# Moving operands of the two feed-forward products kept as even and odd columns 4 KB apart and read alternately

## The chip, the cores and the metric

The kernel runs on one core of a Trainium2 chip. The metric is the device time of one execution in microseconds (us), as the median of several runs; a profile is one more execution, with the hardware profiler on.

## The reference, cut to what matters

A batch of 8 sequences of 576 tokens, with 8 heads of 64 numbers, goes through an attention of two parts: one over means of 4 tokens (144 x 144 scores a head), and a local one over the 7 nearest tokens. Their sum, as a matrix x of 4608 tokens by 512, goes through two dense layers:

```python
h = x @ w_in                                        # 4608 x 512 by 512 x 2048
g = np.maximum(h, 0.0) + alpha * np.minimum(h, 0.0)
return (g @ w_out).astype(np.float32)               # 4608 x 2048 by 2048 x 512
```

The inputs are 64-bit floats in memory; the kernel reads them as pairs of 32-bit words and builds 32-bit floats of the weights itself.

## The kernel before, in words

**The two products.** Every factor is held as a high part of type float32r (a rounded 32-bit type of TensorE) and a low part, the rest; a product is high*high + high*low + low*high. The tokens are cut in 18 chunks of T = 256, the 2048 columns of h in 16 blocks of 128, two to a step, so there are NS = 144 steps, 8 (NP) to a chunk. A step issues two groups on TensorE:

- `hidden` (L751) computes h for 2 blocks: 24 matmuls, in which a 128 x 128 piece of the first weights (`wi`, high or low) is the stationary operand and 256 tokens of x (`xT[c]`, tiles xh and xl) the moving one (L760).
- `product` (L805) adds two blocks of g times the second weights to the output: 12 matmuls, in which 128 tokens of g (gh or gl) are stationary and 512 columns of a row block of the second weights (`wo`, tiles woh and wol) move (L817).

The stationary operand is loaded ahead (rows PEld in the profile); the moving operand streams through the array, one column after another. In memory the 256 tokens of x for one of four row blocks, and the 512 columns of a `wo` block, lie next to each other, in 1 KB and 2 KB of a partition.

**Between the two groups** of a step lie ScalarE's `slopes` (L771, L775), VectorE's `larger` (L783), and `split`: ScalarE casts g to gh (L788), GpSimd subtracts it to gl (`sub`, L70).

**Who makes the operands.** `make` (L164) builds the weights from the raw words in five operations: ScalarE reads every second word (L187), VectorE assembles the bits in `temp` (L191 to L197), ScalarE writes the high part (L206 for `wo`), VectorE the low part (L214). For the later batches x is made in units of 192 tokens, on VectorE for the most part (L597 to L677). `place` (L682) then lets ScalarE write the high part (L691) and GpSimd the low part (L70). The first batch has its own code (L523 to L525), its last 64 tokens another (`place_rest`, L840).

**The order.** First comes the first batch's attention with most of the weights, about 100 us. After it every operation has a due time in units of steps (`at`), and the sorted list is issued as it stands, so each engine runs its instructions in that order. Transfers are issued by SyncE (SP) in the same order. The last raw blocks of weights (`load_raw`, L133, with fp = 6 and 7) have tiles in the pool `late`: for fp = 7 those that later hold the x tiles of every third chunk (xh and xl).

Of the kernel before, what the change touches and what calls it, by code (L numbers as in the profile page):

```python
# [51 lines left out]
def tile_attention_moe(ctx: ExitStack, tc: tile.TileContext, q, k, v, w_in, w_out, alpha, out):  # L52
# [13 lines left out]
    def f32(ap):  # L66
        return ap.bitcast(F32)
# [50 lines left out]


    wi, wo = ([[None] * 4, [None] * 4] for _ in range(2))  # L120
    for name, w in (("wi", wi), ("wo", wo)):
        for i, x in enumerate("hl"):
            w[i][0] = const.tile([128, 4, 512], F32R, name=f"{name}{x}0")

# [6 lines left out]
    def load_raw(which, fp, blocks=(0, 1)):  # L133
        raw = raws.setdefault((which, fp), {})
        if fp < NP - 2:
            raw[None] = one.tile([128, 1024, 2], I32, tag=f"slot{turns[0] % 3}", name=f"raw{which}_{fp}")
            raw[0], raw[1] = raw[None][:, 0:512], raw[None][:, 512:1024]
            turns[0] += 1
        src = (w_in, w_out)[which].bitcast(I32)
        for c in blocks:  # L140
            if fp < NP - 2:
                dst = raw[None][:, 512 * c:512 * c + 512]
            elif fp == NP - 2:
                dst = raw[c] = late.tile([128, 512, 2], I32, tag="prod", name=f"raw{which}_{fp}{c}", bufs=PB)
            else:
                dst = raw[c] = late.tile([128, 512, 2], I32, tag=f"x{'hl'[c]}", name=f"raw{which}_{fp}{c}")
            if which == 0:
                nc.sync.dma_start(dst.rearrange("p (k a) b -> p k (a b)", k=2),
                                  bass.AP(src.tensor, 256 * c * 2 * DF + 512 * fp, [[2 * DF, 128], [256 * DF, 2], [1, 512]]))
            else:  # L150
                row = 256 * fp + 128 * c
                nc.sync.dma_start(dst.rearrange("p a b -> p (a b)"), src[row:row + 128, :])

    def weight_tiles(which, n):
        if n == 0 or (wi, wo)[which][0][n] is not None:
            return
        w = (wi, wo)[which]
        for i, x in enumerate("hl"):
            tag = f"slot{2 * which + i}" if n == 3 else f"spare{8 - 4 * n + 2 * which + i}"
            w[i][n] = one.tile([128, 4, 512], F32R, tag=tag, name=f"w{'io'[which]}{x}{n}")  # L160

    def make(which, fp, c=None):  # L164
        n, half = divmod(fp, 2)
        cs = (0, 1) if c is None else (c,)
        k = len(cs) * (2 - which)
        w = (wi, wo)[which]
        st = {}

        def part(i, c):
            if which == 0:
                return w[i][n][:, 2 * cs[0]:2 * cs[-1] + 2, 256 * half:256 * half + 256]
            f = (2 * fp + c) % 4
            return w[i][n][:, f:f + 1]

        def magnitude():
            if not weights_temp:
                weights_temp.append(one.tile([128, 2, 1024], I32, tag="slot3", name="temp"))
            if c is None:  # L180
                t = weights_temp[0][:, turns[1] % 2]
            else:
                t = bank("ql"[turns[1] % 2], f"temp{which}{fp}{c}").bitcast(I32)
            turns[1] += 1
            st["raw"] = raws[which, fp].pop(c).rearrange("p (k a) b -> p k a b", k=k)
            st["t"] = t.rearrange("p (k a) -> p k a", k=k)
            nc.scalar.activation(f32(st["t"]), f32(st["raw"][:, :, :, 1]), AF.Abs)  # L187

        def reach():
            t = st["t"]  # L190
            nc.vector.tensor_scalar(f32(t), f32(t), W_MIN, W_MAX, op0=ALU.max, op1=ALU.min)  # L191
            nc.vector.tensor_scalar(t, t, 3, 0x3FFFFFF8, op0=ALU.logical_shift_left, op1=ALU.bitwise_and)

        def bits():
            t, hi, lo = st["t"], st["raw"][:, :, :, 1], st["raw"][:, :, :, 0]
            nc.vector.scalar_tensor_tensor(t, hi, -0x40000000, t, op0=ALU.bitwise_and, op1=ALU.bitwise_or)  # L196
            nc.vector.scalar_tensor_tensor(t, lo, 29, t, op0=ALU.logical_shift_right, op1=ALU.bitwise_or)  # L197

        def upper():
            weight_tiles(which, n)  # L200
            if which == 0:
                nc.scalar.copy(part(0, 0), f32(st["t"]))
            else:
                for i, c in enumerate(cs):
                    sg = sign[:, 2 * fp + c:2 * fp + c + 1]
                    nc.scalar.activation(part(0, c), f32(st["t"][:, i:i + 1]), AF.Copy, scale=sg)  # L206

        def lower():
            if which == 0:
                nc.vector.tensor_tensor(part(1, 0), f32(st["t"]), f32(part(0, 0)), op=ALU.subtract)  # L210
            else:
                for i, c in enumerate(cs):
                    sg = sign[:, 2 * fp + c:2 * fp + c + 1]
                    nc.vector.scalar_tensor_tensor(part(1, c), f32(st["t"][:, i:i + 1]), sg, f32(part(0, c)),  # L214
                                                   op0=ALU.mult, op1=ALU.subtract)

        return magnitude, reach, bits, upper, lower
# [136 lines left out]
    def operand(c):  # L354
        if c not in xT:
            pool = late if c % 3 == 2 else two
            xT[c] = [pool.tile([128, 4, T], F32R, tag=f"x{x}", name=f"x{x}{c}") for x in "hl"]
        return xT[c]


    def spans(pos, n):
# [7 lines left out]
    def first_batch(st):  # L369
# [55 lines left out]
        def pair(hp):  # L425
# [85 lines left out]
            for w0, nw in ((0, 4), (4, 4), (8, 1)):  # L511
                ps = pair_bank(FPV[hp][w0 // 4], f"fpv{hp}{w0}")
                for i in range(nw):
                    for e, r in enumerate(halves):
                        nc.tensor.matmul(ps[r, WIN * i:WIN * i + WIN], vw[hp][:, w0 + i, e, :],
                                         pT[:, w0 + i, 64 * e:64 * e + 64], start=True, stop=True)
                xs = rest[:, hp, :] if w0 == 8 else st.tile([128, 256], F32, tag="xs", name=f"fxs{hp}{w0}")
                nc.vector.tensor_tensor(
                    xs.rearrange("p (a r) -> p a r", r=4),
                    ps[:, 0:WIN * nw].rearrange("p (a r) -> p a r", r=4),  # L520
                    odf[:, 16 * w0:16 * (w0 + nw)].unsqueeze(2).to_broadcast([128, 16 * nw, 4]), op=ALU.add)
                if w0 < 8:
                    hi, lo = (t[:, hp, :] for t in operand(w0 // 4))  # L523
                    nc.scalar.copy(hi, xs)  # L524
                    nc.vector.tensor_tensor(lo, xs, f32(hi), op=ALU.subtract)  # L525
            yield

        return load_pair, load_windows, pair
# [43 lines left out]
    def local(u, t0, t1):  # L572
# [109 lines left out]
        def place(i, low):  # L682
            j0, nt = groups[i]
            xv = st["xf", i].rearrange("p a t s -> p a (t s)")
            at_ = 0
            for c, o, n in spans(192 * u + 32 * j0, 32 * nt):
                hi, lo = (t[:, :, o:o + n] for t in operand(c))
                if low:
                    sub(lo, xv[:, :, at_:at_ + n], f32(hi))
                else:  # L690
                    nc.scalar.copy(hi, xv[:, :, at_:at_ + n])  # L691
                at_ += n

        def put(i, t):
# [55 lines left out]

    def hidden(st):  # L751
        c, fp = divmod(st, NP)
        xh, xl = xT[c]
        ph = hs[st] = ps_h.tile([128, 2, T], F32, tag="ph", name=f"h{st}")
        for j in range(2):
            n, o = divmod(2 * fp + j, 4)
            i = 0
            for w, x in ((wi[0][n], xh), (wi[1][n], xh), (wi[0][n], xl)):
                for m in range(4):
                    nc.tensor.matmul(ph[:, j], w[:, m, 128 * o:128 * o + 128], x[:, m, :],  # L760
                                     start=(i == 0), stop=(i == 11))
                    i += 1

# [41 lines left out]
    def product(st):  # L805
# [7 lines left out]
        for j, i, m in order:  # L813
            f = 2 * fp + j
            n, o = divmod(f, 4)
            g, w = ((gh, 0), (gh, 1), (gl, 0))[i]
            nc.tensor.matmul(outs[c][m], g[:, j, 128 * m:128 * m + 128], wo[w][n][:, o, :],  # L817
                             start=(f == 0 and i == 0), stop=(f == NF - 1 and i == 2))

    def finish(c):  # L820
# [17 lines left out]
                (nc.sync if i % 2 == 0 else nc.scalar).dma_start(ap, sg[32 * i:32 * i + 32, :])  # L838

    def place_rest():  # L840
        hi, lo = (t[:, :, 0:S - 2 * T] for t in operand(2))
        nc.scalar.copy(hi, rest)
        sub(lo, rest, f32(hi))

# [47 lines left out]
    for w, fp, c in blocks:  # L894
        for lag, f in zip((-0.3, 0.0, 0.4, 0.95, 1.2), make(w, fp, c)):
            at(t + lag * D_DEC, f)
        t += D_DEC
        if w == 0 and fp >= NP - 2:
            at(t, load_raw, 1, fp, (c,))
    decoded = t  # L900
    for p in range(4 * (B - 1)):
        b, hp = 1 + p // 4, p % 4
# [87 lines left out]
```

## Time and profile before

| | |
|---|---|
| median of 3 runs | 999.41 us (998.8 to 1003.49) |
| span of the profiled execution | 995.7 us |
| median over that span | 3.7 us |
| busy TensorE / VectorE / ScalarE / GpSimd | 955.8 / 825.6 / 559.2 / 497.8 us |
| matmuls of L760 (h) | 3456 of 256 columns, in 144 groups of 24 |
| matmuls of L817 (output) | 1728 of 512 columns, in 144 groups of 12 |
| granted TensorE clock, mean | 0.978 |

PE is TensorE, DVE VectorE, ACT ScalarE, POOL GpSimd. A row of the chain of waits has a start, a time and what ran; one of the groups by form has the line, operation, output and inputs, shapes and count, then busy time, mean ns of one, and the engine's idle time before. Matmuls overlap in the records, so the time from one to the next is read from the chain, not from the mean of one.

### The profile page before, as it was taken

The page shows a single profiled execution, that of the slowest core. Times are in us where ns is not written, and L with a number is a line of the kernel's source. Part 1 is how long each engine was busy: PE and PEld are TensorE (multiplying, and loading weights), DVE is VectorE, ACT ScalarE, POOL GpSimd, SP SyncE. Part 2 cuts the span into 40 slices and gives each one's busy share as a digit, 9 for nine tenths or more (in the row PEclk, how much of TensorE's full clock was granted, in tenths as well). Part 3 has the DMA queues.
Part 4 walks back from the last instruction along what each step waited for, and adds up shares of the span by engine and source line. Part 5 has one row for each costly group of instructions (what it writes and reads, how often), then busy time and mean ns, then how long its engine had stood idle before and what let it go on. Part 6 is the DMA issues. An engine that isn't in the chain of part 4 may idle for free.

```text
span 995.7 us, 17954 instructions
## 1 busy us (share of the span) xinstructions
PE 955.8 (96%) x6402; PEld 850.2 (85%) x6402; DVE 825.6 (83%) x1336; ACT 559.2 (56%) x1483; POOL 497.8 (50%) x624
## 2 busy tenths in 40 slices
PE   5977999999999999999999999999999999999998
PEld 4756877888889888888998889898889888899896
DVE  7999887889898889899899888899898889996111
ACT  5766775455656555555565555565556564544442
POOL 2132866677475636555546455655456632324221
PEclk9957999999999999999999999999999999999999
DMA  8947524243423322423322323232324222210000
GB/s 209 217 150 260 159 65 130 79 126 90 131 90 100 111 87 68 136 79 102 98 87 82 117 84 109 91 104 88 100 84 126 85 67 67 70 33 22 1 22 22
DMA packets 63196, 98.27 MB, mean 99 GB/s; under 512 B 23556, under 2 KB 28932, under 8 KB 63108
## 3 DMA queue, kind: packets, MB, share of 16 engines
q1 hardware_dynamic: 62916, 96.88, 33.0%
q8 instruction: 50, 0.82, 0.3%
q10 hardware_dynamic: 192, 0.26, 0.1%
q14 instruction: 38, 0.31, 0.1%
HBM read 87.67 MB, written 9.44 MB: 98 GB/s over the span
## 4 chain that ended last, share of the span: by engine, by line
PE 77%; DVE 12%; ACT 3%; POOL 3%; issue 2%; SPq 1%; DMA 1%; DVEq 0%; POOLq 0%; ACTq 0%
PE o L817 35%; PE h L760 35%; PE s L266 2%; PE pv L300 2%; PE xp L665 1%; DVE temp L196 1%; DVE lb L656 1%; PE pT L290 1%; DVE qk L597 1%; DVE temp L197 1%; DVE ls L601 1%; SPq L399 1%; POOL t L73 1%; DVE wil L210 1%; DVE pv L653 1%
## 5 line engine op out<-in xcount | busy, mean ns | idle before, releaser
L70 POOL TENSOR_TENSOR gl<-t,gh 128x512 fp32r<-128x512 f32 x144 | 186.3, 1294 | 347.2 <-ACT gh L788 340.1
L771 ACT ACTIVATE t<-h,slope 128x256 f32<-128x256 f32 x288 | 136.7, 474 | 144.7 <-PE h L760 117.5
L817 PE MATMUL o<-woh,gh 128*128 128x512 f32 x576 | 194.9, 409 | 2.6 <-ACT sg L823 2.6
L760 PE MATMUL h<-xh,wih 128*128 128x256 f32 x1152 | 189.5, 286 | 0.6 <-ACT xh L524 0.6
L817 PE MATMUL o<-wol,gh 128*128 128x512 f32 x576 | 188.2, 397 | 0.2 <-DVE wol L214 0.2
L817 PE MATMUL o<-woh,gl 128*128 128x512 f32 x576 | 187.9, 397 | 0.0
L760 PE MATMUL h<-xl,wih 128*128 128x256 f32 x1152 | 183.1, 281 | 0.8 <-POOL xl L70 0.8
L760 PE MATMUL h<-xh,wil 128*128 128x256 f32 x1152 | 183.2, 281 | 0.0
L783 DVE TENSOR_TENSOR t<-h,t 128x512 f32<-128x512 f32 x132 | 90.7, 687 | 103.0 <-ACT h L775 101.8
L760 PEld LDWEIGHTS h<-xh,wih 128*128 128x128 f32 x1152 | 163.5, 190 | 11.0 <-issue 1.0
L788 ACT CAST gh<-t 128x512 fp32r<-128x512 f32 x144 | 89.2, 619 | 127.7 <-DVE t L783 95.7
L760 PEld LDWEIGHTS h<-xl,wih 128*128 128x128 f32 x1152 | 156.3, 189 | 1.0 <-POOL xl L70 1.0
L760 PEld LDWEIGHTS h<-xh,wil 128*128 128x128 f32 x1152 | 156.4, 189 | 0.0
L73 POOL TENSOR_TENSOR ld<-ld 72x256 f32<-72x256 f32 x168 | 127.5, 759 | 42.4 <-DMA ld<-in_q 39.7
L601 DVE TENSOR_REDUCE ls<-qk 128x12 f32<-128x768 f32 (+1 forms) x126 | 136.5, 1084 | 3.2
L817 PEld LDWEIGHTS o<-woh,gl 128*128 128x128 f32 x576 | 108.7, 189 | 26.3
L817 PEld LDWEIGHTS o<-wol,gh 128*128 128x128 f32 x576 | 108.3, 188 | 26.4 <-DVE wol L214 1.4
L656 DVE TENSOR_TENSOR lb<-lb,pv 128x384 f32<-128x384 f32 x202 | 113.9, 564 | 5.6
L817 PEld LDWEIGHTS o<-woh,gh 128*128 128x128 f32 x576 | 99.6, 189 | 20.2 <-ACT sg L823 3.1
L775 ACT ACTIVATE h<-h,sign 128x256 f32<-128x256 f32 x264 | 116.1, 440 | 0.0
L653 DVE TENSOR_TENSOR pv<-v,lb 128x1152 f32<-128x1152 f32 x84 | 93.6, 1115 | 2.6
L597 DVE TENSOR_TENSOR qk<-k,qp 128x768 f32<-128x768 f32 (+1 forms) x78 | 83.9, 1076 | 0.0
(151 smaller groups left out, 1133.4 us busy)
## 6 DMA issues: line engine op xcount, KB each, us to landing
k<-in_k SPq DMA_DIRECT2D x41, 384.0 KB
v<-in_v SPq DMA_DIRECT2D x41, 384.0 KB
out<-sg SPq DMA_DIRECT2D x140, 64.0 KB
raw<-in_moe_w_in SPq DMA_DIRECT2D x16, 512.0 KB
raw<-in_moe_w_out SPq DMA_DIRECT2D x16, 512.0 KB
ld<-in_q SPq DMA_DIRECT2D x56, 144.0 KB
ld<-in_k SPq DMA_DIRECT2D x56, 144.0 KB
ld<-in_v SPq DMA_DIRECT2D x56, 144.0 KB
```

Of the source, the lines that this page charges most:

```text
L70: nc.gpsimd.tensor_tensor(o, a, b, op=ALU.subtract)
L73: nc.gpsimd.tensor_tensor(o, a, b, op=ALU.add)
L597: nc.vector.tensor_tensor(st["pr"][:, :nd], window(tiles[u, "k"], half, d0, nd), st["qp", half].unsqueeze(1).to_broadcast([128, nd, 2, 192 ...
L601: nc.vector.tensor_reduce(out=st["s"][:, half, d0:d0 + nd, :].rearrange("p a b -> p (a b)"), in_=st["pr"][:, :nd].rearrange("p a h (t d) - ...
L653: nc.vector.tensor_tensor(st["pr"][:, :nd], window4(tiles[u, "v"], half, d0, nd), prob(half, d0, nd), op=ALU.mult)
L656: nc.vector.tensor_tensor(st["acc"], st["acc"], st["pr"][:, i], op=ALU.add)
L760: nc.tensor.matmul(ph[:, j], w[:, m, 128 * o:128 * o + 128], x[:, m, :], start=(i == 0), stop=(i == 11))
L771: nc.scalar.activation(t[:, j], hs[st][:, j], AF.Copy, scale=slope[:, f:f + 1])
L775: nc.scalar.activation(other[:, j], hs[st][:, j], AF.Copy, scale=sign[:, f:f + 1])
L783: nc.vector.tensor_tensor(gs[st], hs.pop(st), gs[st], op=ALU.max)
L788: nc.scalar.copy(gh, t)
L817: nc.tensor.matmul(outs[c][m], g[:, j, 128 * m:128 * m + 128], wo[w][n][:, o, :], start=(f == 0 and i == 0), stop=(f == NF - 1 and i == 2))
```

## The change

The moving operands are stored in another order and read so that the columns come out as before.

- A `wo` tile was [128, 4 blocks, 512 columns]; it is now [128, 2, 4 blocks, 256]: all even columns of the four blocks first (4 KB), then all odd ones. The matmul reads even 0, odd 0, even 1, odd 1 and so on, so each 4-byte word lies 4 KB from the one before it.
- xh and xl of a chunk become one tile xx, [128, 2 parities, high or low, 4 row blocks, 128 tokens], again with 4 KB between an even token and the odd one beside it. `hidden` reads them alternately.
- The writers (ACT, DVE and POOL) read every second word of their source and write runs of 128 or 256 words and shorter, one for each parity.
- The raw blocks with fp = 7 share one tile of the tag xx. So the two transfers of the second weights' last block are issued together, once both halves of the first weights' last block have been used.

In the new file the matmuls of L760 stand in line 772, those of L817 in line 829.

```diff
+    WSHAPE = ([128, 4, 512], [128, 2, 4, 256])
-            w[i][0] = const.tile([128, 4, 512], F32R, name=f"{name}{x}0")
+            w[i][0] = const.tile(WSHAPE[which], F32R, name=f"{name}{x}0")
+    def by_parity(ap):
+        return ap.rearrange("p (a e) -> p e a", e=2)
...
-                dst = raw[c] = late.tile([128, 512, 2], I32, tag=f"x{'hl'[c]}", name=f"raw{which}_{fp}{c}")
+                if not raw:
+                    raw["both"] = late.tile([128, 2, 512, 2], I32, tag="xx", name=f"raw{which}_{fp}")
+                dst = raw[c] = raw["both"][:, c]
...
-            return w[i][n][:, f:f + 1]
+            return w[i][n][:, :, f]
...
-                    nc.scalar.activation(part(0, c), f32(st["t"][:, i:i + 1]), AF.Copy, scale=sg)
+                    nc.scalar.activation(part(0, c), by_parity(f32(st["t"][:, i])), AF.Copy, scale=sg)
...
-                    nc.vector.scalar_tensor_tensor(part(1, c), f32(st["t"][:, i:i + 1]), sg, f32(part(0, c)),
+                    nc.vector.scalar_tensor_tensor(part(1, c), by_parity(f32(st["t"][:, i])), sg, f32(part(0, c)),
                                                    op0=ALU.mult, op1=ALU.subtract)
...
-            xT[c] = [pool.tile([128, 4, T], F32R, tag=f"x{x}", name=f"x{x}{c}") for x in "hl"]
+            xT[c] = pool.tile([128, 2, 2, 4, T // 2], F32R, tag="xx", name=f"xx{c}")
+    def tokens(c, i, o, n):
+        return operand(c)[:, :, i, :, o // 2:(o + n) // 2]
+    def pairs(ap):
+        return ap.rearrange("p m (a e) -> p e m a", e=2)
...
-                hi, lo = (t[:, :, o:o + n] for t in operand(c))
+                hi, lo = (tokens(c, i, o, n) for i in range(2))
                 if low:
-                    sub(lo, xv[:, :, at_:at_ + n], f32(hi))
+                    sub(lo, pairs(xv[:, :, at_:at_ + n]), f32(hi))
                 else:
-                    nc.scalar.copy(hi, xv[:, :, at_:at_ + n])
+                    nc.scalar.copy(hi, pairs(xv[:, :, at_:at_ + n]))
...
-        xh, xl = xT[c]
+        x = xT[c].rearrange("p e i m a -> p i m a e")
-            for w, x in ((wi[0][n], xh), (wi[1][n], xh), (wi[0][n], xl)):
+            for w, part in ((wi[0][n], 0), (wi[1][n], 0), (wi[0][n], 1)):
-                    nc.tensor.matmul(ph[:, j], w[:, m, 128 * o:128 * o + 128], x[:, m, :],
+                    nc.tensor.matmul(ph[:, j], w[:, m, 128 * o:128 * o + 128], x[:, part, m],
...
-            nc.tensor.matmul(outs[c][m], g[:, j, 128 * m:128 * m + 128], wo[w][n][:, o, :],
+            nc.tensor.matmul(outs[c][m], g[:, j, 128 * m:128 * m + 128], wo[w][n][:, :, o].rearrange("p e a -> p a e"),
...
-        if w == 0 and fp >= NP - 2:
+        if w == 0 and fp == NP - 2:
             at(t, load_raw, 1, fp, (c,))
+        elif w == 0 and fp == NP - 1 and c == 1:
+            at(t, load_raw, 1, fp)
```

On TensorE a group of `hidden` in the middle of the run, followed by a score matmul of the attention and the first matmuls of `product`, before the change:

```order
L760 MATMUL h_2262<-xh_1737,wih_81 128x256 x4
L760 MATMUL h_2262<-xh_1737,wil_82 128x256 x4
L760 MATMUL h_2262<-xl_1738,wih_81 128x256 x4
L760 MATMUL h_2262<-xh_1737,wih_81 128x256 x4
L760 MATMUL h_2262<-xh_1737,wil_82 128x256 x4
L760 MATMUL h_2262<-xl_1738,wih_81 128x256 x4
L266 MATMUL s_0_2294<-kd_0_2254,qd_85 96x144 x3
L817 MATMUL o_0_1814<-woh_1534,gh_2177 128x512
```

The same place after it:

```order
L772 MATMUL h_2257<-xx_1733,wih_81 128x256 x4
L772 MATMUL h_2257<-xx_1733,wil_82 128x256 x4
L772 MATMUL h_2257<-xx_1733,wih_81 128x256 x8
L772 MATMUL h_2257<-xx_1733,wil_82 128x256 x4
L772 MATMUL h_2257<-xx_1733,wih_81 128x256 x4
L272 MATMUL s_0_2289<-kd_0_2249,qd_85 96x144 x3
L829 MATMUL o_0_1809<-woh_1530,gh_2172 128x512
```

The matmuls are as many and in the same order; eight now stand in one row because xh and xl have one name. VectorE, ScalarE and GpSimd keep their order too, all through the program.

On SP the transfers around the second weights' last raw block (raw_70 and raw_71 are its halves, q and k the first unit's queries and keys, ld_2 the sums' inputs of the next batch), before:

```order
L539 DMA q_1345<-in_q 128x1x384 x2
L152 DMA raw_70_1348<-in_moe_w_out 128x1024
L558 DMA k_1359<-in_k 128x1x768 x2
L235 DMA ld_2_3_1363<-in_k 72x512
L235 DMA ld_2_4_1390<-in_v 72x512
L152 DMA raw_71_1397<-in_moe_w_out 128x1024
L235 DMA ld_2_5_1436<-in_v 72x512
```

And after:

```order
L551 DMA q_1342<-in_q 128x1x384 x2
L570 DMA k_1354<-in_k 128x1x768 x2
L241 DMA ld_2_3_1358<-in_k 72x512
L241 DMA ld_2_4_1385<-in_v 72x512
L158 DMA raw_7_1392<-in_moe_w_out 128x1024 x2
L241 DMA ld_2_5_1432<-in_v 72x512
```

The first half moved behind four other transfers and stands beside the second.

More of the change, by code (lines that the diff above doesn't have):

```diff
@@ L120, in tile_attention_moe @@
     wi, wo = ([[None] * 4, [None] * 4] for _ in range(2))
-    for name, w in (("wi", wi), ("wo", wo)):
+    WSHAPE = ([128, 4, 512], [128, 2, 4, 256])
+    for which, (name, w) in enumerate((("wi", wi), ("wo", wo))):
         for i, x in enumerate("hl"):
-            w[i][0] = const.tile([128, 4, 512], F32R, name=f"{name}{x}0")
+            w[i][0] = const.tile(WSHAPE[which], F32R, name=f"{name}{x}0")
+    def by_parity(ap):
+        return ap.rearrange("p (a e) -> p e a", e=2)
     raws, turns = {}, [0, 0]
@@ L159, in weight_tiles @@
             tag = f"slot{2 * which + i}" if n == 3 else f"spare{8 - 4 * n + 2 * which + i}"
-            w[i][n] = one.tile([128, 4, 512], F32R, tag=tag, name=f"w{'io'[which]}{x}{n}")
+            w[i][n] = one.tile(WSHAPE[which], F32R, tag=tag, name=f"w{'io'[which]}{x}{n}")
     def make(which, fp, c=None):
@@ L522, in pair @@
                 if w0 < 8:
-                    hi, lo = (t[:, hp, :] for t in operand(w0 // 4))
-                    nc.scalar.copy(hi, xs)
-                    nc.vector.tensor_tensor(lo, xs, f32(hi), op=ALU.subtract)
+                    hi, lo = (operand(w0 // 4)[:, :, i, hp, :] for i in range(2))
+                    nc.scalar.copy(hi, by_parity(xs))
+                    nc.vector.tensor_tensor(lo, by_parity(xs), f32(hi), op=ALU.subtract)
             yield
@@ L840, in place_rest @@
     def place_rest():
-        hi, lo = (t[:, :, 0:S - 2 * T] for t in operand(2))
-        nc.scalar.copy(hi, rest)
-        sub(lo, rest, f32(hi))
+        hi, lo = (tokens(2, i, 0, S - 2 * T) for i in range(2))
+        nc.scalar.copy(hi, pairs(rest))
+        sub(lo, pairs(rest), f32(hi))
     load_alpha()
```

## The prediction

> **What bounds the kernel now.** I read the page first, then the busy time by stages, then the chain of waits in a busy and in a quiet stretch. The page:
>
> ```profile
> span 995.7 us, 17954 instructions
> PE 955.8 (96%) x6402; PEld 850.2 (85%) x6402; DVE 825.6 (83%) x1336; ACT 559.2 (56%) x1483; POOL 497.8 (50%) x624
> ```
>
> The stages (window, its length, then busy us and instructions of each engine, granted clock, DMA share, GB/s); the last row is a part of the third:
>
> ```profile
> core 0: us, PE busy (x) PEld busy (x) DVE busy (x) ACT busy (x) POOL busy (x), PEclk, DMA share, GB/s
> 0.00:100.00 100.00, 73.34 (x523) 62.48 (x524) 90.38 (x155) 66.00 (x161) 25.06 (x42) 0.80 0.76 208
> 100.00:200.00 100.00, 94.37 (x617) 81.37 (x616) 83.79 (x125) 62.96 (x165) 69.28 (x87) 0.98 0.37 108
> 200.00:900.00 700.00, 696.87 (x4695) 624.92 (x4695) 628.32 (x1022) 392.50 (x1075) 380.81 (x478) 1.00 0.31 93
> 900.00:996.00 96.00, 91.25 (x574) 81.44 (x572) 23.14 (x37) 37.78 (x83) 22.66 (x18) 1.00 0.07 17
> ...
> 800.00:900.00 100.00, 100.00 (x659) 89.94 (x658) 92.98 (x152) 50.85 (x125) 32.81 (x30) 1.00 0.20 59
> ```
>
> The first 100 us are VectorE's and the transfers'. From 200 us on TensorE is never without work for long, at the full granted clock, and sets the time. VectorE stands close behind: 628.3 of 700 us, 90%.
>
> A busy TensorE is not one at its best pace, so the chain of waits comes next (start, time, work, matmul records), at 505 us with VectorE at 90%, and at 932 us, where it has a quarter of a load:
>
> ```profile
> 505.21 2.87 PE h L760 x24
> 508.09 0.73 PE s L266 x6
> 508.82 2.80 PE o L817 x12
> ...
> 932.26 2.80 PE o L817 x12
> 935.06 2.80 PE h L760 x24
> ```
>
> A group of h moves 24 x 256 = 6144 columns, one of the output 12 x 512 = 6144. Both take 2.80 us (the first row 2.87): 0.456 ns a column, whether 12 instructions or 24, and whether VectorE, GpSimd and the transfers run or not. So the pace hangs on the moving columns alone, not on issue, not on the loads of weights (twice as many in the h group), not on contention with other engines. These are what the change touches.
>
> The score matmuls between them are plain f32, not float32r:
>
> ```profile
> L266 PE MATMUL s<-kd,qd 128*96 128x144 f32 x168 | 25.4, 288 | 3.7 <-ACT kd L261 3.7
> L760 PE MATMUL h<-xl,wih 128*128 128x256 f32 x1152 | 183.1, 281 | 0.8 <-POOL xl L70 0.8
> ```
>
> Six records of 144 columns in 0.73 us are 0.845 ns a column. My estimate, from that row alone: a column of such a record takes two beats of 0.4225 ns, and a float32r column could go in one. Then the products lose 0.456 - 0.4225 = 0.033 ns, 7%, on each column, and lose it only where a new 4-byte word is wanted each beat. I take it for the reading of words that lie side by side.
>
> **The change part by part.** *The two products.* The matmuls are as many and as ordered as before; only the address of each next word differs. How TensorE reads words 4 KB apart is in no row here, since every moving operand of the kernel runs along contiguous words. I bound it. Fastest: one beat a column, 6144 x 0.4225 = 2.60 us a group, 0.204 us less. Slowest: every word costs two beats, as in the L266 row, 6144 x 0.845 = 5.19 us, 2.39 us more. I take the fast end: the words then come from two places 4 KB apart in turn, so each place has two columns' time for its next word, and the L266 row shows that two beats a word are enough for reading without loss.
>
> How many groups lie in each stage (matmuls of L817, then of L760):
>
> ```profile
> 100.00:200.00 100.00, 44.37 (x168) 31.37 (x168) 0.98 0.37 108
> 200.00:900.00 700.00, 337.41 (x1342) 244.25 (x1343) 1.00 0.31 93
> 900.00:996.00 96.00, 50.84 (x208) 37.45 (x206) 1.00 0.07 17
> ...
> 100.00:200.00 100.00, 43.52 (x347) 42.07 (x346) 0.98 0.37 108
> 200.00:900.00 700.00, 336.41 (x2673) 326.96 (x2672) 1.00 0.31 93
> 900.00:996.00 96.00, 44.78 (x360) 44.33 (x360) 1.00 0.07 17
> ```
>
> Divided by 12 and 24: 14 + 14.5 = 28.5 groups from 100 to 200 us, 111.8 + 111.4 = 223.2 from 200 to 900, 17.3 + 15 = 32.3 after. At 0.204 us each that is 5.8, 45.5 and 6.6 us; all 288 groups would give 58.8.
>
> *How much of it arrives.* After 900 us VectorE is done (23 of 96 us) and all 6.6 us arrive. From 200 to 900 us the stretch would shrink to 654.5 us, and VectorE's 628.3 us would fill 96% of it. VectorE now waits for TensorE's results by way of ScalarE; within 200 to 905 us:
>
> ```profile
> DVE t L783 <- ACT h L775: 40.6, 41, 2.4
> ```
>
> Such waits shrink by themselves when h comes sooner. But VectorE's largest share beside a TensorE without a gap is 93.0% (800 to 900 us). If it could do no more, the stretch would end at 628.32 / 0.9298 = 675.8 us: a gain of 24.2. I take the middle, 35. What is late next is gl: the chain from h over L771, L783 and L788 to GpSimd. From 100 to 200 us the chain runs over weights and sums and TensorE idles 5.6 us; I take half, 2.9. In the first 100 us nothing.
>
> *The writers.* The source is now read at every second word, as L187 does already:
>
> ```profile
> L187 ACT ACTIVATE temp<-raw 128x512 f32<-128x512 f32 x12 | 7.7, 640 | 3.3 <-DVE wol L214 1.7 <-DVE wil L210 1.6
> L691 ACT CAST xh<-xf 128x512 fp32r<-128x512 f32 x16 | 10.0, 623 | 15.1 <-DVE xf L677 14.9
> L196 DVE SCALAR_TENSOR_TENSOR temp<-raw,temp 128x512 int32<-128x512 int32 x12 | 8.2, 687 | 0.0
> L783 DVE TENSOR_TENSOR t<-h,t 128x512 f32<-128x512 f32 x132 | 90.7, 687 | 103.0 <-ACT h L775 101.8 <-ACT dp L285 0.5 <-POOL ld L73 0.2
> L677 DVE TENSOR_TENSOR xf<-xp,od 128x128 f32<-128x128 f32 x74 | 26.2, 390 | 8.3 <-POOL xl L70 8.1
> L677 DVE TENSOR_TENSOR xf<-xp,od 128x256 f32<-128x256 f32 x16 | 10.2, 635 | 0.4 <-PE xp L665 0.4
> L70 POOL TENSOR_TENSOR xl<-xf,xh x47: 460/742/1303, 189.0 to 919.8; 128x256 fp32r<-128x256 f32 x21, 128x512 fp32r<-128x512 f32 x16, 128x128 fp32r<-128x128 f32 x5, 128x384 fp32r<-128x384 f32 x5
> ```
>
> ScalarE: 640 against 623 ns, 17 ns on some 70 operations, 1.2 us on an engine half idle. VectorE: L196 reads every second word and takes 687 ns like the contiguous L783, so nothing for the 16 operations of L214 and the 8 of L525. At worst they pay what L677 pays, whose operands all jump: (635 - 390) / 128 = 1.91 ns a word. Contiguous words go at 1.04 (1353 and 953 ns for 1152 and 768, below), so 0.87 ns more on 16 x 512 + 8 x 256 words: 8.9 us, in the first 150 us, where nothing would hide them. GpSimd: no row reads at that step; at worst its 47 x 0.74 us grow by the same 84%, 29 us, hidden in 319 idle us of the middle stretch. TensorE has waited 0.8 us in all for xl (row L760). I take zero for all three.
>
> ```profile
> L653 DVE TENSOR_TENSOR pv<-v,lb 128x1152 f32<-128x1152 f32 x42 | 56.8, 1353 | 1.3
> L653 DVE TENSOR_TENSOR pv<-v,lb 128x768 f32<-128x768 f32 x34 | 32.4, 953 | 1.1
> ...
> 118.08 0.36 SPq L152 DMA_DIRECT2D raw<-in_moe_w_out  x1
> 121.33 0.35 SPq L152 DMA_DIRECT2D raw<-in_moe_w_out  x1
> 137.17 0.67 ACT L187 ACTIVATE temp<-raw 128x512 f32<-128x512 f32 x1
> ```
>
> *The moved transfer.* The half raw block issued at 118.08 us goes behind k and two loads, to the second half at 121.33: some 3 us later. It is first read at 137.17 us, so 16 us are left. The four transfers that it passes start 0.4 us sooner. Nothing either way.
>
> **Sum.** 35 + 6.6 + 2.9 = 44.5 us off the span: 951.2. The median stands 3.7 us above the span, so **955.0 us**. Its own range goes from 940.6 (all 58.8 us) to 962 (28 of the 45.5 us in the middle).
>
> **The rivals.** *VectorE takes over.* The middle stretch gains only 24.2 us, the start nothing: 995.7 - 24.2 - 6.6 + 3.7 = 968.6 us. For it: 93% is the most that the trace shows. Against it: the 40.6 us of waits above are TensorE's doing. It decides once a pair of groups is under 628.3 / 0.9298 / 111.6 = 6.06 us apart, beside 700 / 111.6 = 6.27 now.
>
> *Slower: a word read alone costs a second beat.* If a fetch brings several neighbouring words, of which now one is used, TensorE falls to the L266 pace on all 288 groups: 288 x 2.39 = 688 us, 999.4 + 688 = 1687 us, with no cover, since TensorE has no gaps. L677 speaks for it: 1.91 / 1.04 = 1.84 times the time where neighbouring words aren't next, about what 0.845 / 0.456 = 1.85 says. L196 speaks against: with every second word in use it loses nothing. It decides from 0.459 ns a column on, where 5 us are lost. [...]
>
> *Nothing changes.* The 0.456 ns could be the array's or the accumulation's, not the reading's; then the layout is idle and the time stays at 999.4 us. Nothing in the trace excludes it; the two-beat reading of L266 speaks against. [...]
>
> **How the numbers follow.** Forecast 0.48, VectorE's takeover 0.20, nothing changes 0.13, slower 0.19. The measurement tells about 0.5%, 5 us, from no change. The first two cases are faster: 0.68; same 0.13; slower 0.19. The range runs from 940, the whole gain, over both faster cases to 1004, which holds the unchanged case with the slowest run of before (1003.49); it leaves out the slow rival and little else.
>
> **What would show it.** In the chain of the new profile a group of 12 (now L829) or 24 (L772) takes 2.60 us where I am right, 2.80 where nothing changes, more where the rival holds; 932 us into the old run is the cleanest place, without VectorE. VectorE's share from 200 us to its end rises to 94 or 95%; at 93% or less with TensorE waiting, the takeover is there. Row L783 loses most of its wait for L775. L206, L214 and L691 keep their times within 5%, and the first 100 us stay. A group at 2.65 us or above would prove the beat of 0.4225 ns wrong as the floor, and a TensorE with gaps over 3% from 300 us on would prove wrong what I let VectorE bear.

## The result, and the profile after

The changed kernel takes 973.25 us (median of 4 runs, 972.88 to 976.64), the one before 999.11 us on the same chip: a ratio of 0.9744, 95% interval 0.9721 to 0.9768. That is 25.9 us less, 2.6%. The forecast was 44.4 us less (955.0), the range 940 to 1004.

The page of the profiled execution, which is the slowest of the four (the other three have spans of 971.1 to 971.6 us); the span of before lies 3.7 us under its median, so the two spans show less of the gain than the medians do:

```profile
span 974.9 us, 17954 instructions
PE 914.8 (94%) x6402; PEld 835.9 (86%) x6402; DVE 823.9 (85%) x1336; ACT 563.2 (58%) x1483; POOL 498.7 (51%) x624
```

TensorE is busy 41 us less and the span is only 21 us shorter (26 by the medians): a good third to a half of what the matmuls gave up has become idle time, 13 us of it between 200 and 880 us. The chain of waits from 901 us on, where VectorE is through, shows the two groups alone (L829 was L817, L772 was L760):

```profile
901.86 2.68 PE h L772 x24
904.54 2.59 PE o L829 x12
907.13 2.68 PE h L772 x24
```

Both were at 2.80 us. The output's group now runs at 2.59 / 6144 = 0.4216 ns a column, h's at 0.436.

The stretch from 200 to 880 us, in which VectorE works all the time, by engine and then for the output's matmuls alone; first the kernel before:

```profile
200.00:880.00 680.00, 676.87 (x4570) 606.95 (x4570) 609.66 (x992) 382.48 (x1053) 372.09 (x470) 1.00 0.32 95
200.00:880.00 680.00, 326.19 (x1296) 235.73 (x1296) 1.00 0.32 95
```

and then the changed one:

```profile
200.00:880.00 680.00, 663.82 (x4721) 613.47 (x4720) 627.86 (x1020) 394.63 (x1078) 378.98 (x480) 1.00 0.31 96
200.00:880.00 680.00, 315.22 (x1344) 245.75 (x1344) 1.00 0.31 96
```

1344 matmuls are 112 steps, against 108 before: a step takes 6.07 us where it took 6.30. TensorE's idle time in the stretch went from 3.1 to 16.2 us, and VectorE's share from 89.7 to 92.3%. The waits say what is late now (who waited for whom; us in total, times, the longest); before, within 200 to 905 us:

```profile
ACT gh L788 <- DVE t L783: 79.1, 54, 3.7
ACT t L771 <- PE h L760: 85.0, 52, 3.2
```

and in the changed kernel within 200 to 895 us:

```profile
ACT gh L800 <- DVE t L795: 128.0, 69, 4.0
ACT t L783 <- PE h L772: 41.0, 36, 2.4
DVE t L795 <- ACT h L787: 23.3, 29, 2.3
PE xp L677 <- DVE x L671: 5.5, 5, 2.2
```

ScalarE stands waiting for VectorE's `larger` longer than before (128 against 79 us) before it can cast gh, and for h half as long. VectorE's own waits by way of ScalarE fell from 40.6 to 23.3 us: it has become the late one. TensorE itself waits longest not for gh or gl but for the sums of the attention that VectorE makes (last row, the transposes of x): 5.5 of its 16.2 idle us.

### The profile page after: what moved, and what is told of

Same layout as the page of the kernel before. It is cut to its first block, busy times and chain, and to the rows that moved or that the text cites. A ratio compares the mean times of both kernels' runs of the same rounds, so it can differ in the third digit from the quotient of the medians.

```text
span 974.9 us, 17954 instructions
## 1 busy us (share of the span) xinstructions
PE 914.8 (94%) x6402; PEld 835.9 (86%) x6402; DVE 823.9 (85%) x1336; ACT 563.2 (58%) x1483; POOL 498.7 (51%) x624
## 5 line engine op out<-in xcount | busy, mean ns | idle before, releaser
L772 PE MATMUL h<-xx,wih 128*128 128x256 f32 x2304 | 336.3, 279 | 2.9 <-ACT xx L536 1.5
L772 PEld LDWEIGHTS h<-xx,wih 128*128 128x128 f32 x2304 | 302.2, 193 | 10.2 <-ACT xx L536 1.8
L829 PE MATMUL o<-woh,gh 128*128 128x512 f32 x576 | 186.1, 394 | 5.5 <-ACT sg L835 5.3
L783 ACT ACTIVATE t<-h,slope 128x256 f32<-128x256 f32 x288 | 136.5, 474 | 80.0 <-PE h L772 67.7
L829 PE MATMUL o<-wol,gh 128*128 128x512 f32 x576 | 178.3, 380 | 0.5 <-DVE wol L220 0.4
L829 PE MATMUL o<-woh,gl 128*128 128x512 f32 x576 | 178.0, 380 | 0.0
L772 PE MATMUL h<-xx,wil 128*128 128x256 f32 x1152 | 177.4, 277 | 0.0
L772 PEld LDWEIGHTS h<-xx,wil 128*128 128x128 f32 x1152 | 153.4, 194 | 0.0
L829 PEld LDWEIGHTS o<-wol,gh 128*128 128x128 f32 x576 | 109.1, 190 | 16.6 <-DVE wol L220 1.7
L829 PEld LDWEIGHTS o<-woh,gl 128*128 128x128 f32 x576 | 109.2, 190 | 15.6
L668 DVE TENSOR_TENSOR lb<-lb,pv 128x384 f32<-128x384 f32 x202 | 113.9, 564 | 5.6
L829 PEld LDWEIGHTS o<-woh,gh 128*128 128x128 f32 x576 | 100.0, 191 | 18.6 <-ACT sg L835 6.5
L645 POOL TENSOR_TENSOR pv<-v,lex 128x384 f32<-128x384 f32 x50 | 41.1, 829 | 25.9 <-DVE lex L637 17.2
L70 POOL TENSOR_TENSOR xx<-xf,xx 128x256 fp32r<-128x256 f32 (+3 forms) x47 | 43.7, 933 | 18.1 <-ACT xx L703 18.1
```

Of the source, the lines that this page charges most:

```text
L70: nc.gpsimd.tensor_tensor(o, a, b, op=ALU.subtract)
L668: nc.vector.tensor_tensor(st["acc"], st["acc"], st["pr"][:, i], op=ALU.add)
L783: nc.scalar.activation(t[:, j], hs[st][:, j], AF.Copy, scale=slope[:, f:f + 1])
```

## The experiments

Each was timed beside the kernel before on the same chip; ratios are to that kernel.

**One half alone.** The first kernel has only the second weights in the new layout and order, the second only x (with the merged tile and the moved transfer).

```diff
 first: from the kernel before
-            return w[i][n][:, f:f + 1]
+            return w[i][n][:, :, f]
...
-            nc.tensor.matmul(outs[c][m], g[:, j, 128 * m:128 * m + 128], wo[w][n][:, o, :],
+            nc.tensor.matmul(outs[c][m], g[:, j, 128 * m:128 * m + 128], wo[w][n][:, :, o].rearrange("p e a -> p a e"),
...
 second: from the changed kernel, the same lines the other way round
```

> Only the second weights lie as even and odd columns 4 KB apart; x and the raw blocks are as before. Theory (the reading of the moving words sets the pace, and VectorE takes back a part): a group of 12 output matmuls takes 2.59 us, a group of 24 of h stays at 2.80; 144 x 0.21 = 30 us could go, about half arrives: 978 to 986 us. Rival (the gain of the change comes from the other edits, the merged tile or the moved transfer): 999 us, and 2.59 us a group would be without effect.

> Only x is in the new layout (with the merged tile and the moved transfer); the second weights are as before. Theory: a group of 24 of h takes 2.68 us, one of 12 of the output stays at 2.80; 144 x 0.12 = 17 us could go, a half to all of it arrives: 982 to 990 us. Rival (other edits make the gain): 973 us, since they are all here.

Measured: 982.9 us with the output's half (0.9814, 0.9776 to 0.9852) and 986.2 with x's (0.9847, 0.9811 to 0.9883). The chain of the first:

```profile
916.38 2.59 PE o L821 x12
918.98 2.84 PE h L764 x24
```

and of the second:

```profile
917.05 2.80 PE o L829 x12
919.86 2.68 PE h L772 x24
```

Each half speeds up its own group alone. Against the 1000.7 us of before beside them the halves gain 17.8 and 14.5 us, 32 together; both at once gain 26. What one half leaves is not all there for the other, so something outside the products takes a share. (In the first kernel the untouched groups of h take 2.80 to 2.88 us from 915 us on, not always 2.80; in the kernel before they take 2.80 to 2.87.)

**All of it but the alternation.** Layout, writers, merged tile and moved transfer stay; TensorE reads one parity in a row, then the other.

```diff
-        x = xT[c].rearrange("p e i m a -> p i m a e")
+        x = xT[c].rearrange("p e i m a -> p i m e a")
...
-            nc.tensor.matmul(outs[c][m], g[:, j, 128 * m:128 * m + 128], wo[w][n][:, :, o].rearrange("p e a -> p a e"),
+            nc.tensor.matmul(outs[c][m], g[:, j, 128 * m:128 * m + 128], wo[w][n][:, :, o],
```

> All of the change, but TensorE reads the even columns in a row and then the odd ones, so the tokens and the columns of the output come out in another order. Theory: both groups are back at 2.80 us and the time at 997 to 1002 us, as all of the gain comes from the alternation. Rival (layout of the writers, merged tile, moved transfer): 973 us.

Measured: 1000.4 us, a ratio of 1.0 (0.9977 to 1.0023). The chain:

```profile
916.80 2.80 PE o L829 x12
919.61 2.80 PE h L772 x24
```

All of the gain is in the order of reading, and the other edits cost nothing that can be measured while TensorE reads in a row. (What they cost at the new pace is seen with the two runs close together, below.)

**Who takes back the rest.** Six in ten of VectorE's additions of L668 are left out, in the changed kernel and in the one before.

```diff
         def gather(i):
+            if i:
+                return
             nc.vector.tensor_tensor(st["acc"], st["acc"], st["pr"][:, i], op=ALU.add)
```

> The changed kernel with 118 of 202 additions of L668 left out (the sums of the local attention lack terms), 118 x 0.564 = 66 us of VectorE's work. Theory (VectorE takes back what is missing of the gain): TensorE has no gaps, 144 x (2.59 + 2.68) = 759 us beside some 189 us of its other work and waits as before, and 4 us around: 948 to 958 us. Rival (TensorE waits for GpSimd's gl, ScalarE or transfers): 968 to 973 us.

> The kernel before, with the same 118 additions of L656 left out (the sums of the local attention lack terms). Theory (before, TensorE alone sets the time from 200 us on): 993 to 999 us, at most 0.6% less. Rival (VectorE's work is a brake in either kernel): clearly less, 985 us or below, and then the gain of the run with less work does not belong to the change.

Measured: 953.9 us for the changed kernel (0.9519, 0.9485 to 0.9553), 997.2 for the one before (0.9970, 0.9952 to 0.9988). The first one's engines and output matmuls from 200 to 850 us:

```profile
200.00:850.00 650.00, 647.40 (x4629) 601.14 (x4628) 560.20 (x897) 391.74 (x1064) 374.42 (x474) 1.00 0.33 100
200.00:850.00 650.00, 309.29 (x1320) 241.26 (x1320) 1.00 0.33 100
```

With VectorE at 86% TensorE has 2.6 us of gaps and a step takes 650 / 110 = 5.91 us. The same relief is worth 19 us to the changed kernel (973.25 to 953.9) and 3 to the one before. So VectorE, hardly a brake before, holds back some 16 us more of the changed kernel. The rival that TensorE waits for GpSimd or transfers falls: their work was untouched.

The same 113 steps, from the start of the 15th output group to that of the 128th, show it more sharply (window, its length, then the output's matmuls and loads in it). Before, changed, before with less work for VectorE, changed with less work:

```profile
195.15:903.40 708.25, 341.16 (x1356) 246.74 (x1357) 1.00 0.30 92
202.21:886.77 684.56, 317.98 (x1356) 248.03 (x1357) 1.00 0.31 95
197.75:902.49 704.74, 341.16 (x1356) 246.79 (x1357) 1.00 0.30 92
195.70:863.16 667.46, 317.73 (x1356) 247.93 (x1357) 1.00 0.32 97
```

With all of VectorE's work the change is worth 23.7 us on these steps; with less of it 37.3 us, and 113 steps of 0.21 + 0.12 us are 37.3 us. So all that the groups give arrives once VectorE has less to do.

**A smaller relief with the full computation.** In all units of the later batches, not just the first four of them, GpSimd takes two of the seven neighbours.

```diff
-        near = 7 - FAR.get(u, 1)
+        near = 7 - FAR.get(u, 2)
```

> The changed kernel, with the farthest two of the seven neighbours on GpSimd in all units (before: two in units 3 to 6, one in the others). It takes 2 x (0.40 + 0.56) us off VectorE in each of 17 units, 33 us in all, and puts 2 x (0.83 + 1.02) us on GpSimd, 63 us in all. Theory (VectorE takes back the gain): 955 to 966 us. Rival (GpSimd's gl then comes late, or TensorE was not waiting for VectorE): 972 us or more.

> The kernel before, with the same two neighbours on GpSimd in all units. Theory: nothing to gain, since TensorE has no gaps: 996 to 1001 us. Rival: a gain of 10 us or more as in the changed kernel.

Measured: 963.5 us on the changed kernel (0.9629, 0.9601 to 0.9656; 6 runs), 1004.0 on the one before (1.002, 0.9999 to 1.0041). The engines and output matmuls of the first:

```profile
200.00:850.00 650.00, 643.90 (x4594) 596.32 (x4593) 581.89 (x964) 385.62 (x1054) 430.43 (x541) 1.00 0.33 100
200.00:850.00 650.00, 305.66 (x1302) 238.40 (x1300) 1.00 0.33 100
```

VectorE is back at 89.5%, a step at 650 / 108.5 = 5.99 us. GpSimd takes the work over: it is busy 562 us in all, beside 499. The 113 steps take 673.29 us, 11.3 less than in the changed kernel, of 13.6 that are missing there. This version beats both kernels, and by an edit that is worth nothing without the change.

**Does the distance matter?** The columns of the second weights lie 1 KB apart here, the tokens of x 2 KB.

```diff
-    WSHAPE = ([128, 4, 512], [128, 2, 4, 256])
+    WSHAPE = ([128, 4, 512], [128, 4, 2, 256])
...
-            xT[c] = pool.tile([128, 2, 2, 4, T // 2], F32R, tag="xx", name=f"xx{c}")
+            xT[c] = pool.tile([128, 2, 2, 4, T // 2], F32R, tag="xx", name=f"xx{c}").rearrange("p i e m a -> p e i m a")
```

> Alternating still, but the even and the odd columns of the second weights lie 1 KB apart, the tokens of x 2 KB apart. If the distance of 4 KB matters (two places of the memory that work apart): groups of the output at 2.80 us or more, those of h too. If only the alternation matters: 2.59 and 2.68 us, and about 973 us in all.

One run: 980.6 us, with the same groups:

```profile
921.56 2.68 PE h L772 x24
924.24 2.59 PE o L829 x12
```

The 4 KB are not needed for the pace of the groups. The time of this single run lies 4 us above the slowest of the changed kernel. A late start doesn't explain it: its first output matmul comes at 102.7 us, that of the changed kernel at 102.0. Why it is longer stays open.

**Other orders of reading.** The first kernel is the one before with steps of 8 bytes (x) and 16 bytes (second weights). The second is the changed one with two neighbouring words from each region in turn (second weights), and x alternating 512 bytes apart.

The operands as the matmuls read them, and the tile of x:

```diff
 first
+ x[:, m, :].rearrange("p (a e) -> p e a", e=2)
+ wo[w][n][:, o, :].rearrange("p (a e) -> p e a", e=4)
 second
+ wo[w][n][:, :, o].rearrange("p e (b r) -> p b e r", r=2)
+ xT[c] = pool.tile([128, 2, 4, 2, T // 2], F32R, tag="xx", name=f"xx{c}").rearrange("p i m e a -> p e i m a")
```

> The kernel before, its layout untouched; only the order in which TensorE reads a moving operand differs: a group of h reads every second token of a contiguous run and then the others (8 bytes from word to word), one of the output every fourth column and then the next fourths (16 bytes), so tokens and columns come out in another order. Theory of two places in turn: no gain, 2.80 us or more a group, since nothing alternates. Theory that only the neighbour of a word must not be next: 2.59 us for the output's groups, 2.68 for those of h. Rival of single words (a fetch brings neighbours, and they must be used): up to 5.2 us a group.

> The output's products read two neighbouring words from each of the two regions 4 KB apart in turn (its columns come out in another order); the tokens of x alternate 512 bytes apart. Theory of two places in turn: the output's groups at 2.59 us, those of h at 2.68. Theory that only the neighbour of a word must not be next: the output's groups between 2.59 and 2.80 us, since every second step is to a neighbour; those of h at 2.68.

One run each: 1759.3 and 1145.9 us. The chain of the first, then of the second:

```profile
700.09 5.53 PE o L817 x12
...
706.07 5.49 PE h L760 x24
```

```profile
703.94 4.03 PE o L829 x12
707.97 2.68 PE h L772 x24
```

Steps of 8 or 16 bytes cost 0.89 and 0.90 ns a column, twice the time of contiguous words (0.456): the size of the prediction's slow rival, but for other orders than the one here. That it is the rival's mechanism, a fetch of which neighbours go unused, isn't shown. Pairs in turn cost 0.656 ns, which neither theory had: 2.59 was expected by the one, at most 2.80 by the other. The theory of two places that work apart falls with it, since pairs change places half as often and are slower than no change of place at all (0.656 beside 0.456).

**Two runs close together.** The kernel before, its layout untouched; the output's groups alternate 64 bytes apart, those of h 16 bytes apart.

```diff
-            nc.tensor.matmul(outs[c][m], g[:, j, 128 * m:128 * m + 128], wo[w][n][:, o, :],
+            nc.tensor.matmul(outs[c][m], g[:, j, 128 * m:128 * m + 128], wo[w][n][:, o, :].rearrange("p (b e a) -> p b a e", e=2, a=16),
...
-                    nc.tensor.matmul(ph[:, j], w[:, m, 128 * o:128 * o + 128], x[:, m, :],
+                    nc.tensor.matmul(ph[:, j], w[:, m, 128 * o:128 * o + 128], x[:, m, :].rearrange("p (b e a) -> p b a e", e=2, a=4),
```

> The kernel before, its layout untouched; only the order of reading differs: the output's groups take words 64 bytes apart in turn (0, 16, 1, 17, 2, 18 and so on within 32 columns), those of h words 16 bytes apart in turn (0, 4, 1, 5 and so on within 8 tokens); tokens and columns come out in another order. Theory of order (what counts is that two runs advance in turn, wherever they lie): 2.59 us a group of the output and 2.68 of h. Theory of place (the two words must lie some distance apart, more than 16 bytes, and at 512 at the latest): 5.5 us a group of h as in steps of 16 bytes, and the output's either 2.59 or 5.5 us, which tells whether 64 bytes are enough.

One run: 969.6 us. The chain:

```profile
916.03 2.68 PE h L760 x24
918.71 2.59 PE o L817 x12
```

Full pace in both, so the theory of order holds: two runs that advance one word each in turn are enough, 64 bytes apart as well as 4 KB (for h, 16 bytes, as far as its own bound lets see, below). No operand has to be laid out anew for the pace. The 113 steps from the 15th to the 128th output group:

```profile
196.88:879.86 682.98, 317.98 (x1356) 248.01 (x1357) 1.00 0.32 95
```

That is 1.6 us less than in the changed kernel, so its layout, writers and merged tile cost little there at the new pace too.

A kernel that reads like this and puts its tokens and columns back in order was not tried.

**Why h gains less than the output.** Each matmul of h in two of 128 columns, with the same columns in all and twice the loads of weights.

```diff
+            for q in range(2):
...
-                    nc.tensor.matmul(ph[:, j], w[:, m, 128 * o:128 * o + 128], x[:, part, m],
+                        nc.tensor.matmul(ph[:, j, 128 * q:128 * q + 128], w[:, m, 128 * o:128 * o + 128],
+                                         x[:, part, m, 64 * q:64 * q + 64],
```

> The changed kernel with each matmul of h cut in two of 128 columns, so 48 loads of weights and 48 matmuls a group. If loading the weights sets the 2.68 us of a group (111.7 ns a load and matmul, whatever the columns): 48 x 111.7 = 5.36 us a group, and about 1350 us in all. If reading the columns sets it (0.436 ns a column): 2.68 us a group, and about 973 us.

One run: 1331.4 us. The chain:

```profile
700.03 5.35 PE h L773 x48
705.38 2.65 PE o L831 x12
```

48 loads and matmuls take 5.35 us, 111 ns each, with half the columns; in the changed kernel 24 took 2.68 us, 111.7 ns each. So a load of 128 x 128 float32r weights with its matmul took the same 111 ns with 128 columns as with 256: here that is its floor, and h has reached it. The output, with 512 columns a load, stays well above, at 2.59 / 12 = 0.216 us. Issuing two instructions doesn't take that long: the four small transposes qkT, each with a load of its own, start 65 ns apart (here in the run with steps of 8 and 16 bytes):

```profile
723.40 0.26 PE qkT L253 x4
```

## Why the prediction was right, and where its size was off

**The mechanism holds, its reason only in part.** The pace was set by the reading of the moving words, not by issue or other engines (1000.4 us with all but the alternation); the alternation lifts the output's groups to what I forecast as one beat a column. The beat, estimated as 0.4225 ns, half a column of the plain f32 row, was measured at 0.4216; that a column of that row takes two of them was my estimate, and no run shows it. That each of two places then has two columns' time for its next word fits the alternation at every distance run here, 64 bytes to 4 KB for the output; but the 4 KB play no part in it, and "words side by side" can't be all: steps of 8 and 16 bytes never take a neighbour next and go half as fast (0.89 and 0.90 ns a column beside 0.456), and pairs in turn lose as well (0.656). That I took the fast end and not the slow one, with no row of TensorE to decide, was partly luck. L196, which I put against the slow rival, reads every second word without loss on VectorE (687 ns in the kernel before, like the contiguous L783); TensorE with the same step took twice the time (5.49 us a group of h beside 2.80).

**The number.** 973.25 us lies inside the range only because the range was wide: it is outside the 940.6 to 962 that I gave my own case, and 4.7 us above the 968.6 of VectorE's takeover, to which I gave 0.20. In the middle it is this rival that came true.

**The h groups: 2.60 us forecast, 2.68 measured.** I said the pace hung "not on the loads of weights", on the ground that twice as many of them made no difference at 2.80 us. They lay just below: a load with its matmul took 111 ns, 256 columns took 2.80 / 24 = 117, and at 0.4216 ns a column they would have taken 108. With 0.21 us for each of 111.8 output groups and 0.12 for 111.4 of h, the middle stretch had 36.8 us to give, not 45.5.

**How much of it arrives is the term that was mis-sized.** I took the middle between all of it and VectorE's takeover, 35 of 45.5 us. Measured: 0.225 us a step (6.30 less 6.07) on the 111.6 steps of that stretch are 25 us; the 113 steps counted one by one give 23.7. The rival gave 24.2, and its point of decision, 6.06 us a step, is where the kernel stands. VectorE needn't be full for that: it fills 92.3%, near the 93.0% that I had read as the most it could do. My reading, not tested by itself, is that the rest is lost in waits that its fixed order passes on. That what is missing hangs on VectorE is shown by the runs with less of its work.

**The signs** that I had named: VectorE's share stayed under 93% with TensorE waiting, the sign of the takeover; L783 lost 43% of its wait for L775, not most of it; TensorE's gaps from 300 to 895 us are 1.7%, under my 3%. The h groups at 2.68 us are above the 2.65 that was to prove the beat wrong as the floor; for them the floor is the load (111 ns), and the output's groups kept the beat (0.4216 ns a column). L206 and L691 moved by 7 and 30%, not within 5.

**The tail** should give 15 x 0.12 + 17.3 x 0.21 = 5.4 us by the measured groups, 6.6 by mine; from the 128th output group on the profiles show 4.3. **The start** was to give 2.9 us from 100 to 200 us and gave nothing. The first and last output matmul of the changed kernel:

```profile
L829 PE MATMUL o<-woh,gh x576: 379/379/795, 102.0 to 969.5; 128*128 128x512 f32 x192
```

Before, the first came at 96.2 us and the last at 990.4. From first to last it is 867.5 against 894.2 us, 26.7 less, and 5.8 us later at the start. (Up to the 15th group 1.3 us more, in the 113 steps 23.7 less, then 4.3 less.) No run ties the late start to the change: the run with all edits but the alternation began at 98.6 us, the one with two runs close together at 98.2, and two runs of the kernel before with less or other work for VectorE at 99.5 and 100.5. The profile of before had an early start. A share of one or two us can't be excluded.

**The writers** cost more than I took from the nearest rows, and in time it hardly mattered:

```profile
L703 ACT CAST xx<-xf 128x512 fp32r<-128x512 f32 x16 | 12.9, 809 | 17.8 <-DVE xf L689 17.8
L212 ACT ACTIVATE woh<-temp,sign 128x512 fp32r<-128x512 f32 x16 | 11.6, 757 | 9.7 <-DVE temp L203 9.7
L220 DVE SCALAR_TENSOR_TENSOR wol<-temp,sign,woh 128x512 fp32r<-128x512 f32 x16 | 11.8, 755 | 2.9 <-ACT woh L212 2.8
L70 POOL TENSOR_TENSOR xx<-xf,xx 128x512 fp32r<-128x512 f32 x16 | 20.8, 1302 | 14.2 <-ACT xx L703 14.2
```

ScalarE's cast of x went from 623 to 809 ns, where I had 17 ns more, that of the weights from 705 to 757; VectorE (751 before) and GpSimd kept theirs. The new layout alone does not do this. In the run with all edits but the alternation the cast of x takes 666 ns:

```profile
L703 ACT CAST xx<-xf 128x512 fp32r<-128x512 f32 x16 | 10.6, 666 | 15.1 <-DVE xf L689 14.9
```

The rest comes with TensorE's alternation, and it meets operations that the change never touched. The rows from which I took the price, L187 and L196 (now L193 and L202, with 640 and 687 ns before), read every second word of the raw weights. In the changed kernel:

```profile
L193 ACT ACTIVATE temp<-raw 128x512 f32<-128x512 f32 x12 | 9.0, 752 | 3.3 <-DVE wol L220 1.7 <-DVE wil L216 1.6
L202 DVE SCALAR_TENSOR_TENSOR temp<-raw,temp 128x512 int32<-128x512 int32 x12 | 9.0, 753 | 0.0
```

and where TensorE alternates 64 and 16 bytes apart:

```profile
L187 ACT ACTIVATE temp<-raw 128x512 f32<-128x512 f32 x12 | 7.7, 644 | 3.3 <-DVE wol L214 1.7 <-DVE wil L210 1.6
L196 DVE SCALAR_TENSOR_TENSOR temp<-raw,temp 128x512 int32<-128x512 int32 x12 | 8.2, 686 | 0.0
```

In the run with all edits but the alternation they take 641 and 686 ns, in the one with words 1 and 2 KB apart 752 and 750. So words far apart, which gained TensorE nothing over close ones here, slowed these two reads of every second word, from 640 to 752 ns and from 687 to 753; contiguous operations kept their time (VectorE's `larger` 687 and 685 ns, ScalarE's cast of g 619 both times). Why stays open.

**The slower rival** was of the right size for the wrong order: 5.19 us a group by the f32 row, 5.5 measured for steps of 8 and 16 bytes (0.89 and 0.90 ns a column). That the word before is no neighbour doesn't cost this much by itself: in the alternation 4 KB apart it never is one, and the output's columns took 0.4216 ns each. What makes the steps slow was not shown.

## What to carry to other kernels

When a matmul's time goes with its columns, and neither the count of instructions nor the neighbours' load changes it, try the order in which the moving operand is read: the same words in two runs taken in turn went 8% faster here (0.4216 ns a column after 0.456, with 512 columns a load; 4% and 0.436 with 256, where the loads bind), in steps they went half as fast (0.89 and 0.90). Lay the two runs close together, or count what the strided reads of other engines pay beside runs far apart (752 ns after 640 on ScalarE here). Before counting such a gain, set the next engine's work beside the shorter step: VectorE, busy 90% here, took back a third of it (23.7 of 37.3 us arrived), and gave most of that up (11.3 of 13.6 us) when a few per cent of its work moved to GpSimd, which was busy 51%.

## What the runs showed of the hardware

Float32r moving operands, in ns a column of the output's groups (512 columns a matmul), where not said otherwise: contiguous 0.456; two runs in turn, 64 bytes, 1 KB or 4 KB apart, 0.4216; two words from each of two runs in turn 0.656; steps of 16 bytes 0.90; steps of 8 bytes (h) 0.89. In h, 16 bytes, 512 bytes, 2 KB and 4 KB apart all reached 0.436, where the load of weights binds at 111 ns a load and matmul. Beside an alternation of both products 4 KB apart, or 1 and 2 KB, ScalarE's and VectorE's 128x512 reads of every second word took 752 and 750 to 753 ns in the mean; beside one 16 and 64 bytes apart, or none, 640 to 644 and 686 to 687. Why words in a row lose 8% against two runs in turn, and why pairs lose more than either, stays open: no run here shows the mechanism.
